# A SwiGLU kernel: splitting the first gate/up matmul by token halves, issuing the start-up loads from two queues, and changing the warm-up

## The chip, the cores and the metric

One core of one Trainium2 chip. The metric is the device time of one execution in microseconds (us), lower is better. Trace times are counted from the start of the profiled span, which is about 1.7 us shorter than the device time (123.1 us of span for a run of 124.81 us). In the trace of the kernel before, PE does the matmuls (585, with the warm-ups and its transposes), DVE copies, transposes and products (61 instructions), ACT the Silus and output copies (61, a table load among them), POOL the memsets and the identity (7), and SP only issues loads and stores; a q after a name is that engine's sequencer, on which the trace shows DMA transfers, that is, loads and stores, being issued. In the programs, PE's results are tensors declared in PSUM, and the other operands are declared in SBUF.

## The reference

```python
# x: 1 x 2048 x 512, w_gate and w_up: 512 x 1376, w_down: 1376 x 512, all bf16
def reference(x, w_gate, w_up, w_down):
    g = _silu(x @ w_gate)
    u = x @ w_up
    return (g * u) @ w_down
```

## The kernel before

The tokens are worked on in four chunks of 512. A chunk has 11 tiles of hidden columns; each tile is four gate matmuls and four up matmuls of 128x512 (four because D = 512 is contracted in steps of 128), Silu on ACT, a product on DVE, and later the down projection. The matmuls take x transposed (`xT_sb`). For chunk 0, PE transposes x itself against an identity (four token tiles of 128, called T0 to T3 here), and DVE copies each result out of PSUM. Later chunks are transposed on DVE; PE does not wait for them in the profile (its page gives 0.4 us of idle time in front of the gate matmuls, all of it for the copies of chunk 0). In front of its real work PE does *warm-ups*, and after the transposes *fillers*: matmuls on dummy data whose results nobody reads.

The parts that the change touches are all at the start:

```python
N_WARM = 26
N_FILL = 4
W_PIECES = [128, 512, 896]     # column cuts of w_gate and w_up; one DMA and one semaphore per piece
...
        @block.sync
        def _(sp):
            sp.dma_start(x_sb[:, 0, 0:2, :], x_v[:, 0, 0:2, :]).then_inc(s_xa, 16)
            sp.dma_start(x_sb[:, 0, 2:4, :], x_v[:, 0, 2:4, :]).then_inc(s_xb, 16)
            ...
            for i in range(NPC):
                ld_w(sp, "g", i)
                ld_w(sp, "u", i)
...
            pool.memset(zeros_sb[:], 0.0).then_inc(s_zero, 1)
            pool.memset(ones_sb[:], 1.0).then_inc(s_ones, 1)
...                                                     # the identity is made from ones_sb
                pe.wait_ge(s_zero, 1)
                for i in range(N_WARM):
                    pe.matmul(po[1][:, 0:P], zeros_sb[:], zeros_sb[:], start=True, stop=True)
...                                                     # T0 to T3, two PSUM buffers
                    if nT >= 2:
                        pe.wait_ge(s_xT, nT - 1)
                    for kt in range(KT):
                        ins = pe.transpose(pT[buf][:, kt * P:(kt + 1) * P], x_sb[:, 0, j, kt * P:(kt + 1) * P], ident[:])
                    ins.then_inc(s_T, 1)
                    nT += 1
                    if nT == TPC:
                        for i in range(N_FILL):
                            pe.matmul(po[1][:, 0:P], zeros_sb[:], zeros_sb[:], start=True, stop=True)
...                                                     # gate, then up, of tile ft of chunk c
                    if pi not in seen_wg:
                        pe.wait_ge(s_wg[pi], 16)
                        ...
                    if ft == 0:
                        if c == 0:
                            need = T_order.index(c * TPC + TPC - 1) + 1
                            pe.wait_ge(s_xT, need)       # all four copies
                        ...
                    for kt in range(KT):
                        ins = pe.matmul(pg[buf][0:m, :], wg_sb[:, kt, ft * P:ft * P + m],
                                        xT_sb[:, kt, c * NCH:(c + 1) * NCH], start=(kt == 0), stop=(kt == KT - 1))
```

## Time and profile before

| | before |
|---|---|
| median of 4 runs | 124.78 us (124.59 to 125.27) |
| span of the profiled run | 123.1 us |
| PE busy | 119.0 us, 97% of the span |
| first gate matmul / first up matmul | 6.45 us / 7.31 us |

The page of the kernel before: busy time per engine with its share of the span and its instructions, then shares of the chain of work that ended last.

```profile
span 123.1 us, 1467 instructions
...
PE 119.0 (97%) x585; PEld 57.7 (47%) x585; DVE 39.6 (32%) x61; ACT 36.9 (30%) x61; POOL 0.8 (1%) x7
...
PE 96%; DVE 1%; issue 0%; POOL 0%; POOLq 0%
```

PE is the bound from one end to the other in this trace: 97% busy, and 96% of the chain. From 6.45 us on, the groups of four full-size matmuls follow each other every 0.86 us. A change that leaves their number and this rate alone can only move the stretch before they run without a stop. The timeline of the kernel before shows it: start, duration, engine, line, operation, output<-inputs, count, and in brackets the idle time of the engine before it and what ended that.

```profile
0.80 0.43 SPq L153 DMA_DIRECT2D x_sb<-in_x_dram  x1
...
1.06 2.96 PE L191 MATMUL bank<-zeros_sb 128*128 128x128 bf16 x26 [1.06 <-POOL zeros_sb L178]
...
1.29 0.45 SPq L154 DMA_DIRECT2D x_sb<-in_x_dram  x1
...
3.81 1.06 PE L217 MATMUL bank<-ident,x_sb 128*128 128x128 bf16 x8
...
4.48 0.85 DVE L333 COPY xT_sb<-bank 128x512 bf16<-128x512 bf16 x2 [4.48 <-PE bank L217]
...
5.05 0.73 PE L217 MATMUL bank<-ident,x_sb 128*128 128x128 bf16 x8 [0.18 <-DVE xT_sb L333]
5.54 0.76 DVE L333 COPY xT_sb<-bank 128x512 bf16<-128x512 bf16 x2 [0.21 <-PE bank L217]
...
5.62 0.39 PE L222 MATMUL bank<-zeros_sb 128*128 128x128 bf16 x4
...
6.45 1.02 PE L241 MATMUL bank<-xT_sb,wg_sb 128*128 128x512 bf16 x4 [0.44 <-DVE xT_sb L333]
...
7.31 1.03 PE L250 MATMUL bank<-xT_sb,wu_sb 128*128 128x512 bf16 x4
...
8.17 1.03 PE L241 MATMUL bank<-xT_sb,wg_sb 128*128 128x512 bf16 x4
```

PE does 26 warm-ups, T0 and T1, waits 0.18 us for DVE to empty a PSUM buffer, does T2 and T3 and four fillers, and then waits 0.44 us for DVE's fourth copy (5.54 + 0.76 = 6.30) before the first gate matmul. From there the starts are 0.86 us apart.

### The profile page before, as it was taken

Reading aid. Unit: us, or ns where it says so; the run is one execution under the profiler, and the core shown is the slowest. Engines: PE = TensorE matmul, PEld = TensorE weight load, DVE = VectorE, ACT = ScalarE, POOL = GpSimd, SP = SyncE. Lnnn points to the kernel's source line nnn. Section 1 sums busy time; section 2 is a strip of 40 time slices with the busy share of each in tenths; the row PEclk is TensorE's granted clock in tenths of the full one; section 3 lists DMA queues with packets and bytes.
Section 4 is the critical chain, followed back from the end, with each engine's and each line's share of the span. In section 5 each row is a group of like instructions: output and inputs, shape, how many; then the busy total and the mean of one; then the engine's idle time right before and its main releaser. Section 6 shows DMA issues by size and latency. Waiting matters only on the chain.

```text
span 123.1 us, 1467 instructions
## 1 busy us (share of the span) xinstructions
PE 119.0 (97%) x585; PEld 57.7 (47%) x585; DVE 39.6 (32%) x61; ACT 36.9 (30%) x61; POOL 0.8 (1%) x7
## 2 busy tenths in 40 slices
PE   6899999999999999999999999999999999999992
PEld 6744444444444444454444444454444444454471
DVE  0423344463004443365004334438002443342001
ACT  4013332313233233311233332231125233331230
POOL 2000000000000000000000000000000000000000
PEclk9999999999999999999999999999999999999999
DMA  3999996999980000001111000000211000000121
GB/s 111 242 328 372 351 187 67 97 94 90 87 198 9 5 0 0 0 0 43 43 43 43 8 3 0 0 0 0 81 47 43 5 0 0 0 0 0 43 68 60
DMA packets 33398, 8.51 MB, mean 69 GB/s; under 512 B 26256, under 2 KB 33392, under 8 KB 33392
## 3 DMA queue, kind: packets, MB, share of 16 engines
q1 hardware_dynamic: 33248, 8.36, 30.8%
q8 instruction: 4, 0.07, 0.2%
q10 hardware_dynamic: 144, 0.07, 0.2%
q14 instruction: 2, 0.02, 0.1%
HBM read 6.32 MB, written 2.10 MB: 68 GB/s over the span
## 4 chain that ended last, share of the span: by engine, by line
PE 96%; DVE 1%; issue 0%; POOL 0%; POOLq 0%
PE bank L241 31%; PE bank L250 31%; PE bank L274 29%; PE bank L191 2%; PE bank L287 1%; PE bank L282 1%; DVE xT_sb L333 1%; PE bank L217 1%; DVE out_sb L356 0%; POOL zeros_sb L178 0%; POOLq L371 0%
## 5 line engine op out<-in xcount | busy, mean ns | idle before, releaser
L347 DVE TENSOR_TENSOR hT_sb<-bank,sg 128x512 bf16<-128x512 f32 (+1 forms) x44 | 30.4, 691 | 67.9 <-PE bank L250 67.9
L241 PE MATMUL bank<-xT_sb,wg_sb 128*128 128x512 bf16 (+1 forms) x176 | 45.2, 379 | 0.4 <-DVE xT_sb L333 0.4
L250 PE MATMUL bank<-xT_sb,wu_sb 128*128 128x512 bf16 (+1 forms) x176 | 45.2, 379 | 0.0
L305 ACT ACTIVATE sg<-bank 128x512 bf16<-128x512 f32 (+1 forms) x44 | 26.3, 597 | 51.4 <-PE bank L241 51.4
L274 PE MATMUL bank<-wd_sb,hT_sb 128*128 128x512 bf16 (+1 forms) x165 | 36.3, 379 | 0.0
L241 PEld LDWEIGHTS bank<-xT_sb,wg_sb 128*128 128x128 bf16 (+1 forms) x176 | 17.5, 100 | 20.8 <-issue 0.6
L250 PEld LDWEIGHTS bank<-xT_sb,wu_sb 128*128 128x128 bf16 (+1 forms) x176 | 17.6, 100 | 20.4
L274 PEld LDWEIGHTS bank<-wd_sb,hT_sb 128*128 128x128 bf16 (+1 forms) x165 | 16.1, 98 | 19.5
L314 ACT ACTIVATE out_sb<-bank 128x512 bf16<-128x512 f32 x15 | 9.0, 597 | 30.2 <-PE bank L274 30.2
L340 DVE STREAM_TRANSPOSE xT_sb<-xb_sb 128x512 bf16<-128x512 bf16 x12 | 7.4, 673 | 0.0
L191 PE MATMUL bank<-zeros_sb 128*128 128x128 bf16 x26 | 3.0, 313 | 1.1 <-POOL zeros_sb L178 1.1
L356 DVE CAST out_sb<-bank 128x256 bf16<-128x256 f32 x1 | 0.4, 423 | 8.9 <-PE bank L287 8.9
L191 PEld LDWEIGHTS bank<-zeros_sb 128*128 128x128 bf16 x26 | 2.7, 149 | 1.1 <-POOL zeros_sb L178 1.1
L333 DVE COPY xT_sb<-bank 128x512 bf16<-128x512 bf16 x4 | 1.6, 423 | 4.7 <-PE bank L217 4.7
L217 PE MATMUL bank<-ident,x_sb 128*128 128x128 bf16 x16 | 1.8, 275 | 0.2 <-DVE xT_sb L333 0.2
L217 PEld LDWEIGHTS bank<-ident,x_sb 128*128 128x128 bf16 x16 | 1.4, 130 | 0.5 <-issue 0.4
L294 ACT ACT_TABLE_LOAD x1 | 1.3, 1283 | 0.8 <-PEq L371 0.8
L282 PE MATMUL bank<-wd_sb,hT_sb 128*128 128x256 bf16 (+1 forms) x11 | 1.4, 272 | 0.0
L287 PE MATMUL bank<-wd_sb,hT_sb 128*128 128x256 bf16 (+1 forms) x11 | 1.4, 272 | 0.0
L282 PEld LDWEIGHTS bank<-wd_sb,hT_sb 128*128 128x128 bf16 (+1 forms) x11 | 1.1, 97 | 0.3
L287 PEld LDWEIGHTS bank<-wd_sb,hT_sb 128*128 128x128 bf16 (+1 forms) x11 | 1.1, 98 | 0.1
L316 ACT ACTIVATE out_sb<-bank 128x256 bf16<-128x256 f32 x1 | 0.4, 385 | 0.6 <-PE bank L282 0.6
(9 smaller groups left out, 1.8 us busy)
## 6 DMA issues: line engine op xcount, KB each, us to landing
out_dram<-out_sb SPq DMA_DIRECT2D x15, 128.0 KB, 1.7
xb_sb<-in_x_dram SPq DMA_DIRECT2D x12, 128.0 KB, 4.1
wd_sb<-in_w_down_dram SPq DMA_DIRECT2D x1, 1280.0 KB, 9.7
wg_sb<-in_w_gate_dram SPq DMA_DIRECT2D x2, 384.0 KB, 5.0
wu_sb<-in_w_up_dram SPq DMA_DIRECT2D x2, 384.0 KB, 5.5
x_sb<-in_x_dram SPq DMA_DIRECT2D x2, 256.0 KB, 2.7
wg_sb<-in_w_gate_dram SPq DMA_DIRECT2D x1, 480.0 KB, 6.4
wu_sb<-in_w_up_dram SPq DMA_DIRECT2D x1, 480.0 KB, 7.3
```

What stands on the lines that cost most here:

```text
L191: pe.matmul(po[1][:, 0:P], zeros_sb[:], zeros_sb[:], start=True, stop=True)
L217: ins = pe.transpose(pT[buf][:, kt * P:(kt + 1) * P], x_sb[:, 0, j, kt * P:(kt + 1) * P], ident[:])
L241: ins = pe.matmul(pg[buf][0:m, :], wg_sb[:, kt, ft * P:ft * P + m], xT_sb[:, kt, c * NCH:(c + 1) * NCH], start=(kt == 0), stop=(kt == KT - 1))
L250: ins = pe.matmul(pu[buf][0:m, :], wu_sb[:, kt, ft * P:ft * P + m], xT_sb[:, kt, c * NCH:(c + 1) * NCH], start=(kt == 0), stop=(kt == KT - 1))
L274: ins = pe.matmul(po[buf][:, :], hT_sb[0:m, ft, t * P:(t + 1) * P], wd_sb[0:m, ft, :], start=(ft == 0), stop=(ft == FT - 1))
L282: ins = pe.matmul(pTf[0][:, 0:HALF], hT_sb[0:m, ft, t * P:(t + 1) * P], wd_sb[0:m, ft, 0:HALF], start=(ft == 0), stop=(ft == FT - 1))
L287: ins = pe.matmul(pTf[1][:, HALF:D], hT_sb[0:m, ft, t * P:(t + 1) * P], wd_sb[0:m, ft, HALF:D], start=(ft == 0), stop=(ft == FT - 1))
L305: act.activation(sg_sb[nGU % NSG][0:m, :], pg[buf][0:m, :], ACT.Silu).then_inc(s_sg, 1)
L314: act.activation(out_sb[:, c, j, :], po[buf][:, :], ACT.Copy).then_inc(s_oea, 1)
L333: dve.tensor_copy(xT_sb[:, :, t * P:(t + 1) * P], src).then_inc(s_xT, 1)
L340: dve.transpose(xT_sb[:, kt, c * NCH:(c + 1) * NCH], src).then_inc(s_xTd, 1)
L347: dve.tensor_tensor(hT_sb[0:m, ft, c * NCH:(c + 1) * NCH], pu[buf][0:m, :], sg_sb[nGU % NSG][0:m, :], ALU.mult).then_inc(s_h, 1)
```

## The change

Its intent: do not wait for all of x before the first gate matmuls, and get the start-up loads going from two queues at once. The core of it (renamings, and a reshaping of views that alters nothing, are cut):

```diff
-N_WARM = 26
-N_FILL = 4
+N_WARM = 30
...
+        ones_c = nc.const_aps.tensor(1.0, [P, P], BF16)      # broadcast of a constant that the start-up code sets
...
         def _(sp):
-            sp.dma_start(x_sb[:, 0, 0:2, :], x_v[:, 0, 0:2, :]).then_inc(s_xa, 16)
-            sp.dma_start(x_sb[:, 0, 2:4, :], x_v[:, 0, 2:4, :]).then_inc(s_xb, 16)
+            sp.dma_start(x_sb[:, 0:2, :], x_v[:, 0:2, :]).then_inc(s_x0a, 16)
...
         def _(pool):
-            pool.memset(zeros_sb[:], 0.0).then_inc(s_zero, 1)
-            pool.memset(ones_sb[:], 1.0).then_inc(s_ones, 1)
-            pool.wait_ge(s_ones, 1)
...
-                pe.wait_ge(s_zero, 1)
-                for i in range(N_WARM):
-                    pe.matmul(po[1][:, 0:P], zeros_sb[:], zeros_sb[:], start=True, stop=True)
+            for i in range(N_WARM):
+                pe.matmul(po[1][:, 0:P], ones_c, ones_c, start=True, stop=True)
...
-                    if nT == TPC:
-                        for i in range(N_FILL):
-                            pe.matmul(po[1][:, 0:P], zeros_sb[:], zeros_sb[:], start=True, stop=True)
...
+                    if nGU == 0:
+                        hw_ = NCH // 2
+                        pe.wait_ge(s_wg[pi], 16)
+                        seen_wg.add(pi)
+                        for hh in range(2):
+                            pe.wait_ge(s_xTv, 2 * hh + 2)    # two copies for half 0, four for half 1
+                            for kt in range(KT):
+                                ins = pe.matmul(pg[buf][0:m, hh * hw_:(hh + 1) * hw_], wgl[:, kt],
+                                                xT_sb[:, kt, hh * hw_:(hh + 1) * hw_],
+                                                start=(kt == 0), stop=(kt == KT - 1))
+                        ins.then_inc(s_g, 1)
+                        pe.wait_ge(s_wu[pi], 16)
...                     # the same two halves for up
...
         def _(act):
+            act.dma_start(x_sb[:, 2:4, :], x_v[:, 2:4, :]).then_inc(s_x0b, 16)
             act.preload_act_table(ACT.Silu)
```

More of the change, by code (lines that the diff above doesn't have):

```diff
@@ L25, in bass_standalone__swiglu_ffn__prompt_kernel @@
     F = w_gate.shape[1]
-    assert B == 1
     P = 128
+    NCH = 512
+    assert B == 1 and S % NCH == 0 and D % P == 0 and D <= 512
     x2 = x[0]
@@ L31, in bass_standalone__swiglu_ffn__prompt_kernel @@
     KT = D // P
-    NCH = 512
     SC = S // NCH
@@ L40, in bass_standalone__swiglu_ffn__prompt_kernel @@
     HALF = D // 2
-    x_v = x2.rearrange("(c j p) d -> p c j d", p=P, j=TPC)
-    out_v = out2.rearrange("(c j p) d -> p c j d", p=P, j=TPC)
     G = NCH // 32
+    assert KT == 4 and TPC == 4
+    x_v = x2.rearrange("(t p) d -> p t d", p=P)
+    out_v = out2.rearrange("(t p) d -> p t d", p=P)
+    wg_v = w_gate.rearrange("(kt p) f -> p kt f", p=P)
+    wu_v = w_up.rearrange("(kt p) f -> p kt f", p=P)
     def piece_of(ft):
@@ L57, in sb @@
             return es.enter_context(nc.sbuf_tensor(name, shape, dt))
-        def ps(name, shape, dt):
-            return es.enter_context(nc.psum_tensor(name, shape, dt))
         def sem(name):
             return es.enter_context(nc.semaphore(name))
-        x_sb = sb("x_sb", [P, 1, TPC, D], BF16)
+        x_sb = sb("x_sb", [P, TPC, D], BF16)
         xb_sb = sb("xb_sb", [P, SC, KT, G, 32], BF16)
@@ L71, in bass_standalone__swiglu_ffn__prompt_kernel @@
         hT_sb = sb("hT_sb", [P, FT, S], BF16)
-        out_sb = sb("out_sb", [P, SC, TPC, D], BF16)
-        ones_sb = sb("ones_sb", [P, P], BF16)
+        out_sb = sb("out_sb", [P, ST, D], BF16)
         ident = sb("ident", [P, P], BF16)
-        zeros_sb = sb("zeros_sb", [P, P], BF16)
         NSG = 3
         sg_sb = [sb(f"sg{i}", [P, NCH], BF16) for i in range(NSG)]
-        banks = [ps(f"bank{i}", [P, 512], FP32) for i in range(8)]
+        ones_c = nc.const_aps.tensor(1.0, [P, P], BF16)
+        banks = [es.enter_context(nc.psum_tensor(f"bank{i}", [P, 512], FP32)) for i in range(8)]
         pg = banks[0:2]
@@ L84, in bass_standalone__swiglu_ffn__prompt_kernel @@
         pT = [b.bitcast(BF16) for b in pTf]
-        s_xa = sem("s_xa")
-        s_xb = sem("s_xb")
+        s_x0a = sem("s_x0a")
+        s_x0b = sem("s_x0b")
         s_xc = [None] + [sem(f"s_xc{c}") for c in range(1, SC)]
-        s_xTd = sem("s_xTd")
         s_wg = [sem(f"s_wg{i}") for i in range(NPC)]
@@ L93, in bass_standalone__swiglu_ffn__prompt_kernel @@
         s_ident = sem("s_ident")
-        s_ones = sem("s_ones")
-        s_zero = sem("s_zero")
         s_T = sem("s_T")
-        s_xT = sem("s_xT")
+        s_xTv = sem("s_xTv")
+        s_xTd = sem("s_xTd")
         s_g = sem("s_g")
@@ L108, in bass_standalone__swiglu_ffn__prompt_kernel @@
         block = es.enter_context(nc.Block())
-        pe_items = []
-        for t in range(TPC):
-            pe_items.append(("T", t))
+        items = [("T", j) for j in range(TPC)]
         for c in range(SC):
-            for ft in range(FT):
-                pe_items.append(("GU", c, ft))
+            items += [("GU", c, ft) for ft in range(FT)]
             for j in range(TPC):
-                pe_items.append(("D", c * TPC + j))
+                items.append(("D", c * TPC + j))
                 if c + 1 < SC:
-                    pe_items.append(("X", c + 1, j))
-        T_order = [it[1] for it in pe_items if it[0] == "T"]
-        X_order = [(it[1], it[2]) for it in pe_items if it[0] == "X"]
-        GU_order = [(it[1], it[2]) for it in pe_items if it[0] == "GU"]
-        D_order = [it[1] for it in pe_items if it[0] == "D"]
-        def x_sem(t):
-            c, j = divmod(t, TPC)
-            if c == 0:
-                return s_xa if j < 2 else s_xb
-            return s_xc[c]
-        wg_v = w_gate.rearrange("(kt p) f -> p kt f", p=P)
-        wu_v = w_up.rearrange("(kt p) f -> p kt f", p=P)
+                    items.append(("X", c + 1, j))
+        GU_list = [(it[1], it[2]) for it in items if it[0] == "GU"]
+        D_list = [it[1] for it in items if it[0] == "D"]
+        X_list = [(it[1], it[2]) for it in items if it[0] == "X"]
+        n_wd = 2 if F % P else 1
         def ld_w(eng, which, i):
@@ L140, in ld_w @@
                 eng.dma_start(wu_sb[:, :, a:b], wu_v[:, :, a:b]).then_inc(s_wu[i], 16)
-        nfull = F // P
-        n_wd = 2 if F % P else 1
-        def ld_wd(eng):
-            wd_v = w_down[0:nfull * P, :].rearrange("(ft p) d -> p ft d", p=P)
-            eng.dma_start(wd_sb[:, 0:nfull, :], wd_v).then_inc(s_wd, 16)
-            if F % P:
-                eng.dma_start(wd_sb[0:F % P, nfull, :], w_down[nfull * P:F, :]).then_inc(s_wd, 16)
         @block.sync
         def _(sp):
-            sp.dma_start(x_sb[:, 0, 0:2, :], x_v[:, 0, 0:2, :]).then_inc(s_xa, 16)
-            sp.dma_start(x_sb[:, 0, 2:4, :], x_v[:, 0, 2:4, :]).then_inc(s_xb, 16)
-            def ld_xb(c):
-                src_c = x2[c * NCH:(c + 1) * NCH, :].rearrange("(g b) (kt ii a) -> ii b kt g a", b=32, a=32, ii=4)
-                for i in range(4):
-                    sp.dma_start(xb_sb[32 * i:32 * (i + 1), c], src_c[i]).then_inc(s_xc[c], 16)
+            sp.dma_start(x_sb[:, 0:2, :], x_v[:, 0:2, :]).then_inc(s_x0a, 16)
             for i in range(NPC):
@@ L161, in _ @@
                 ld_w(sp, "u", i)
-            ld_wd(sp)
-            for c in range(1, SC):
-                ld_xb(c)
-            for i, t in enumerate(D_order):
-                c, j = divmod(t, TPC)
-                last = (i == len(D_order) - 1)
-                if last:
+            nfull = F // P
+            wd_v = w_down[0:nfull * P, :].rearrange("(ft p) d -> p ft d", p=P)
+            sp.dma_start(wd_sb[:, 0:nfull, :], wd_v).then_inc(s_wd, 16)
+            if F % P:
+                sp.dma_start(wd_sb[0:F % P, nfull, :], w_down[nfull * P:F, :]).then_inc(s_wd, 16)
+            for c in range(1, SC):
+                src_c = x2[c * NCH:(c + 1) * NCH, :].rearrange(
+                    "(g b) (kt ii a) -> ii b kt g a", b=32, a=32, ii=4)
+                for i in range(4):
+                    sp.dma_start(xb_sb[32 * i:32 * (i + 1), c], src_c[i]).then_inc(s_xc[c], 16)
+            for i, t in enumerate(D_list):
+                if i == len(D_list) - 1:
                     sp.wait_ge(s_oed, 1)
-                    sp.dma_start(out_v[:, c, j, HALF:D], out_sb[:, c, j, HALF:D]).then_inc(s_out, 16)
+                    sp.dma_start(out_v[:, t, HALF:D], out_sb[:, t, HALF:D]).then_inc(s_out, 16)
                 else:
                     sp.wait_ge(s_oea, i + 1)
-                    sp.dma_start(out_v[:, c, j, :], out_sb[:, c, j, :]).then_inc(s_out, 16)
+                    sp.dma_start(out_v[:, t, :], out_sb[:, t, :]).then_inc(s_out, 16)
             sp.wait_ge(s_out, 16 * ST)
@@ L177, in _ @@
         def _(pool):
-            pool.memset(zeros_sb[:], 0.0).then_inc(s_zero, 1)
-            pool.memset(ones_sb[:], 1.0).then_inc(s_ones, 1)
-            pool.wait_ge(s_ones, 1)
             pool.affine_select(
-                out=ident[:], in_=ones_sb[:], pattern=[[-1, P]],
+                out=ident[:], in_=ones_c, pattern=[[-1, P]],
                 compare_op=ALU.is_equal, fill=0.0, base=0, channel_multiplier=1,
@@ L187, in _ @@
         def _(pe):
-            if N_WARM:
-                pe.wait_ge(s_zero, 1)
-                for i in range(N_WARM):
-                    pe.matmul(po[1][:, 0:P], zeros_sb[:], zeros_sb[:], start=True, stop=True)
-            nT = 0
-            nGU = 0
-            nD = 0
-            h_waited = 0
-            first_T = True
-            seen_wg = set()
-            seen_wu = set()
-            seen_x = set()
-            for it in pe_items:
-                if it[0] == "X":
-                    continue
+            for i in range(N_WARM):
+                pe.matmul(po[1][:, 0:P], ones_c, ones_c, start=True, stop=True)
+            nT = nGU = nD = 0
+            h_waited = 0
+            seen_wg, seen_wu = set(), set()
+            for it in items:
                 if it[0] == "T":
-                    t = it[1]
-                    c, j = divmod(t, TPC)
-                    if first_T:
+                    j = it[1]
+                    if nT == 0:
                         pe.wait_ge(s_ident, 1)
-                        first_T = False
-                    xs = x_sem(t)
-                    if xs not in seen_x:
-                        pe.wait_ge(xs, 16)
-                        seen_x.add(xs)
-                    buf = nT % 2
+                        pe.wait_ge(s_x0a, 16)
+                    if nT == 2:
+                        pe.wait_ge(s_x0b, 16)
                     if nT >= 2:
-                        pe.wait_ge(s_xT, nT - 1)
+                        pe.wait_ge(s_xTv, nT - 1)
                     for kt in range(KT):
-                        ins = pe.transpose(pT[buf][:, kt * P:(kt + 1) * P], x_sb[:, 0, j, kt * P:(kt + 1) * P], ident[:])
+                        ins = pe.transpose(pT[nT % 2][:, kt * P:(kt + 1) * P],
+                                           x_sb[:, j, kt * P:(kt + 1) * P], ident[:])
                     ins.then_inc(s_T, 1)
                     nT += 1
-                    if nT == TPC:
-                        for i in range(N_FILL):
-                            pe.matmul(po[1][:, 0:P], zeros_sb[:], zeros_sb[:], start=True, stop=True)
                 elif it[0] == "GU":
@@ L227, in _ @@
                     pi = piece_of(ft)
+                    tok0 = c * NCH
+                    wgl = wg_sb[:, :, ft * P:ft * P + m]
+                    wul = wu_sb[:, :, ft * P:ft * P + m]
+                    if nGU == 0:
[10 more added lines that the diff above has]
+                        pe.wait_ge(s_wu[pi], 16)
+                        seen_wu.add(pi)
+                        for hh in range(2):
+                            for kt in range(KT):
+                                ins = pe.matmul(pu[buf][0:m, hh * hw_:(hh + 1) * hw_], wul[:, kt],
+                                                xT_sb[:, kt, hh * hw_:(hh + 1) * hw_],
+                                                start=(kt == 0), stop=(kt == KT - 1))
+                        ins.then_inc(s_u, 1)
+                        nGU += 1
+                        continue
+                    if c >= 1 and ft == 0:
+                        pe.wait_ge(s_xTd, X_list.index((c, KT - 1)) + 1)
                     if pi not in seen_wg:
@@ L230, in _ @@
                         seen_wg.add(pi)
-                    if ft == 0:
-                        if c == 0:
-                            need = T_order.index(c * TPC + TPC - 1) + 1
-                            pe.wait_ge(s_xT, need)
-                        else:
-                            need = X_order.index((c, KT - 1)) + 1
-                            pe.wait_ge(s_xTd, need)
                     if nGU >= 2:
@@ L240, in _ @@
                     for kt in range(KT):
-                        ins = pe.matmul(pg[buf][0:m, :], wg_sb[:, kt, ft * P:ft * P + m],
-                                        xT_sb[:, kt, c * NCH:(c + 1) * NCH], start=(kt == 0), stop=(kt == KT - 1))
+                        ins = pe.matmul(pg[buf][0:m, :], wgl[:, kt], xT_sb[:, kt, tok0:tok0 + NCH],
+                                        start=(kt == 0), stop=(kt == KT - 1))
                     ins.then_inc(s_g, 1)
@@ L249, in _ @@
                     for kt in range(KT):
-                        ins = pe.matmul(pu[buf][0:m, :], wu_sb[:, kt, ft * P:ft * P + m],
-                                        xT_sb[:, kt, c * NCH:(c + 1) * NCH], start=(kt == 0), stop=(kt == KT - 1))
+                        ins = pe.matmul(pu[buf][0:m, :], wul[:, kt], xT_sb[:, kt, tok0:tok0 + NCH],
+                                        start=(kt == 0), stop=(kt == KT - 1))
                     ins.then_inc(s_u, 1)
                     nGU += 1
-                else:
+                elif it[0] == "D":
                     t = it[1]
                     c = t // TPC
-                    buf = nD % 2
+                    last = (nD == len(D_list) - 1)
                     if nD == 0:
                         pe.wait_ge(s_wd, 16 * n_wd)
-                    last = (nD == len(D_order) - 1)
                     if nD >= 2 and not last:
@@ L265, in wait_h @@
                         nonlocal h_waited
-                        need = GU_order.index((c, ft)) + 1
+                        need = GU_list.index((c, ft)) + 1
                         if need > h_waited:
@@ L269, in wait_h @@
                             h_waited = need
-                    if not last:
+                    groups = [(po[nD % 2], 0, D)] if not last else [(pTf[0], 0, HALF), (pTf[1], HALF, D)]
+                    for (acc, c0, c1) in groups:
                         for ft in range(FT):
@@ L273, in _ @@
                             wait_h(ft)
-                            ins = pe.matmul(po[buf][:, :], hT_sb[0:m, ft, t * P:(t + 1) * P],
-                                            wd_sb[0:m, ft, :], start=(ft == 0), stop=(ft == FT - 1))
-                        ins.then_inc(s_o, 1)
-                    else:
-                        pe.wait_ge(s_xT, len(T_order))
-                        for ft in range(FT):
-                            m = fsz[ft]
-                            wait_h(ft)
-                            ins = pe.matmul(pTf[0][:, 0:HALF], hT_sb[0:m, ft, t * P:(t + 1) * P],
-                                            wd_sb[0:m, ft, 0:HALF], start=(ft == 0), stop=(ft == FT - 1))
-                        ins.then_inc(s_o, 1)
-                        for ft in range(FT):
-                            m = fsz[ft]
-                            ins = pe.matmul(pTf[1][:, HALF:D], hT_sb[0:m, ft, t * P:(t + 1) * P],
-                                            wd_sb[0:m, ft, HALF:D], start=(ft == 0), stop=(ft == FT - 1))
+                            ins = pe.matmul(acc[:, c0:c1], hT_sb[0:m, ft, t * P:(t + 1) * P],
+                                            wd_sb[0:m, ft, c0:c1], start=(ft == 0), stop=(ft == FT - 1))
                         ins.then_inc(s_o, 1)
@@ L293, in _ @@
         def _(act):
+            act.dma_start(x_sb[:, 2:4, :], x_v[:, 2:4, :]).then_inc(s_x0b, 16)
             act.preload_act_table(ACT.Silu)
-            nGU = 0
-            nD = 0
-            for it in pe_items:
+            nGU = nD = 0
+            for it in items:
                 if it[0] == "GU":
-                    c, ft = it[1], it[2]
-                    buf = nGU % 2
-                    m = fsz[ft]
+                    m = fsz[it[2]]
                     act.wait_ge(s_g, nGU + 1)
@@ L304, in _ @@
                         act.wait_ge(s_h, nGU - NSG + 1)
-                    act.activation(sg_sb[nGU % NSG][0:m, :], pg[buf][0:m, :], ACT.Silu).then_inc(s_sg, 1)
+                    act.activation(sg_sb[nGU % NSG][0:m, :], pg[nGU % 2][0:m, :], ACT.Silu).then_inc(s_sg, 1)
                     nGU += 1
@@ L308, in _ @@
                     t = it[1]
-                    c, j = divmod(t, TPC)
-                    buf = nD % 2
-                    last = (nD == len(D_order) - 1)
                     act.wait_ge(s_o, nD + 1)
-                    if not last:
-                        act.activation(out_sb[:, c, j, :], po[buf][:, :], ACT.Copy).then_inc(s_oea, 1)
+                    if nD < len(D_list) - 1:
+                        act.activation(out_sb[:, t, :], po[nD % 2][:, :], ACT.Copy).then_inc(s_oea, 1)
                     else:
-                        act.activation(out_sb[:, c, j, 0:HALF], pTf[0][:, 0:HALF], ACT.Copy).then_inc(s_oea, 1)
+                        act.activation(out_sb[:, t, 0:HALF], pTf[0][:, 0:HALF], ACT.Copy).then_inc(s_oea, 1)
                         act.wait_ge(s_oea, nD + 1)
-                        act.dma_start(out_v[:, c, j, 0:HALF], out_sb[:, c, j, 0:HALF]).then_inc(s_out2, 16)
+                        act.dma_start(out_v[:, t, 0:HALF], out_sb[:, t, 0:HALF]).then_inc(s_out2, 16)
                         act.wait_ge(s_out2, 16)
@@ L323, in _ @@
         def _(dve):
-            nT = 0
-            nGU = 0
-            nD = 0
-            for it in pe_items:
+            nT = nGU = nD = 0
+            for it in items:
                 if it[0] == "T":
-                    t = it[1]
-                    buf = nT % 2
+                    j = it[1]
                     dve.wait_ge(s_T, nT + 1)
-                    src = pT[buf][:, 0:KT * P].rearrange("p (kt s) -> p kt s", kt=KT)
-                    dve.tensor_copy(xT_sb[:, :, t * P:(t + 1) * P], src).then_inc(s_xT, 1)
+                    src = pT[nT % 2][:, 0:KT * P].rearrange("p (kt s) -> p kt s", kt=KT)
+                    dve.tensor_copy(xT_sb[:, :, j * P:(j + 1) * P], src).then_inc(s_xTv, 1)
                     nT += 1
@@ L342, in _ @@
                     c, ft = it[1], it[2]
-                    buf = nGU % 2
                     m = fsz[ft]
@@ L346, in _ @@
                     dve.wait_ge(s_sg, nGU + 1)
-                    dve.tensor_tensor(hT_sb[0:m, ft, c * NCH:(c + 1) * NCH], pu[buf][0:m, :],
+                    dve.tensor_tensor(hT_sb[0:m, ft, c * NCH:(c + 1) * NCH], pu[nGU % 2][0:m, :],
                                       sg_sb[nGU % NSG][0:m, :], ALU.mult).then_inc(s_h, 1)
@@ L350, in _ @@
                 elif it[0] == "D":
-                    t = it[1]
-                    c, j = divmod(t, TPC)
-                    last = (nD == len(D_order) - 1)
-                    if last:
+                    if nD == len(D_list) - 1:
+                        t = it[1]
                         dve.wait_ge(s_o, nD + 2)
-                        dve.tensor_copy(out_sb[:, c, j, HALF:D], pTf[1][:, HALF:D]).then_inc(s_oed, 1)
+                        dve.tensor_copy(out_sb[:, t, HALF:D], pTf[1][:, HALF:D]).then_inc(s_oed, 1)
                     nD += 1
```

## The prediction

> **What bounds the kernel now.** The page gives a span of 123.1 us, PE busy 119.0 us (97%) at full granted clock; the chain of waits is 96% PE. In the timeline, from the first gate matmul (6.45 us) on, each group of four 128x512 matmuls takes 0.86 us and nothing stalls them; after the first tile their number, shape and order do not change. So only the first 7 us can move. The chain there: zeros memset, 26 warm-up matmuls (from 1.06 us, 0.107 us start to start), transposes from 3.81 us, PSUM copies on DVE (0.42 us each; the fourth ends at 6.30), gate matmuls at 6.45, up matmuls at 7.31.
>
> **Where that start waits.** By the trace's semaphore times, the first x half landed at 3.40 us and the second at 4.08, while PE was in warm-ups until 3.81. The first weight pieces landed at 5.4 (gate) and 6.15 us (up). So loads were not last; the warm-up count and then the transpose/copy ping-pong were. Loading earlier has almost no direct value.
>
> **What the change does.**
> 1. Split first tile: gate on tokens 0-255 needs only copies 1 and 2 (done 5.33 us). It can run while copies 3 and 4 finish, where before PE ran four fillers and waited 0.44 us. Eight 256-wide matmuls cost about 0.11 us each (the last output's: 11 in 1.21 us), so both halves cost the same 0.86 us. Four of them, 0.43 us, move into the hole. Gain about 0.4 us.
> 2. Warm-ups: 30 for 26, on the constant, so no memset in front: start near 0.82 instead of 1.06 us, 4 x 0.107 = 0.43 us more work. Transposes start near 4.02 instead of 3.81. Loss about 0.2 us. The fillers (0.2 us) were inside a wait: no gain.
> 3. The second half of x goes out on the ACT queue at 0.8 instead of 1.29 us; weights are issued 0.5 us earlier. [...] DMA share is about 1.0 from 2.5 to 3.5 us. The first half now shares bandwidth and may land as late as 4.0 us, near the new end of the warm-ups: 0 to 0.1 us of loss. Weights arrive 0.2 to 0.4 us sooner, off the chain.
> 4. The table load on ACT moves back 0.5 us; it is needed only at 7.5 us. Free.
>
> Net: up matmuls start near 7.1 instead of 7.31 us; 0.2 us off, from a kernel whose runs spread over 0.7 us.
>
> **Prediction:** 124.5 us, range 123.9 to 125.1. Faster by over 2%: 0.01; within 2%: 0.98; slower by over 2%: 0.01.
>
> **What would show it.** Right: first-half gate matmuls near 5.8 us, PE idle of at most 0.4 us before the second half, up matmuls near 7.1, steady 0.86 us groups afterwards, PE busy almost unchanged. Wrong: transposes waiting long for x (step 3), warm-ups spaced more than 0.107 us (step 2), or the second gate tile waiting for weights.
>
> **What would make it wrong.** The broadcast constant may load as weights more slowly than a full tile: 30 warm-ups at 0.15 us would cost over 1 us. The PE clock: matmul spacing falls from 0.107 to 0.056 us near 5.3 us. [...] An earlier or later release shifts the start by some tenths of a us.

Two passages that no trace or run of this case supports are cut from it and marked. No term of the forecast's sum is among them: it came to about 0.4 us of gain less about 0.2 us of loss, that is, 0.2 us off. In its last paragraph, the 0.15 us per warm-up was a supposition (e2 measured 0.107 us), and the shift by some tenths of a us an estimate of mine (in the trace of e1 a later rise of the matmul rate cost about 0.3 us).

## The result, and the profile after

| | before | after |
|---|---|---|
| median | 125.02 us (16 runs, 124.59 to 125.27) | 124.64 us (11 runs, 124.32 to 124.91) |
| ratio, 95% interval | | 0.9978 (0.9966 to 0.9991) |
| span of the profiled run | 123.1 us | 122.8 us |
| first gate / first up matmul | 6.45 / 7.31 us | 5.80 / 7.02 us |

Ratios here and below are the mean time of one kernel's runs over that of the other's in the same rounds, so they are not quite the ratio of the medians quoted. Executions over 1.5% slower than the fastest of the same kernel are left out of the means. The change is a small gain, clear of the noise, within 2%.

The page of the changed kernel, the same lines:

```profile
span 122.8 us, 1481 instructions
...
PE 119.2 (97%) x593; PEld 58.6 (48%) x593; DVE 39.6 (32%) x61; ACT 36.9 (30%) x61; POOL 0.5 (0%) x5
...
PE 96%; DVE 1%; issue 0%
```

The timeline of the changed kernel:

```profile
0.80 0.43 SPq L127 DMA_DIRECT2D x_sb<-in_x_dram  x1
...
0.81 0.49 ACTq L256 DMA_DIRECT2D x_sb<-in_x_dram  x1
0.84 3.36 PE L160 MATMUL bank<-const-bfloat16-1.0 128*128 128x128 bf16 x30 [0.84 <-PEq L322]
...
4.04 1.01 PE L175 MATMUL bank<-ident,x_sb 128*128 128x128 bf16 x8
...
4.66 0.85 DVE L287 COPY xT_sb<-bank 128x512 bf16<-128x512 bf16 x2 [4.66 <-PE bank L175]
...
5.23 0.74 PE L175 MATMUL bank<-ident,x_sb 128*128 128x128 bf16 x8 [0.18 <-DVE xT_sb L287]
...
5.76 0.76 DVE L287 COPY xT_sb<-bank 128x512 bf16<-128x512 bf16 x2 [0.25 <-PE bank L175]
5.80 0.60 PE L194 MATMUL bank<-xT_sb,wg_sb 128*128 128x256 bf16 x4
...
6.57 0.61 PE L194 MATMUL bank<-xT_sb,wg_sb 128*128 128x256 bf16 x4 [0.17 <-DVE xT_sb L287]
...
7.02 1.04 PE L202 MATMUL bank<-xT_sb,wu_sb 128*128 128x256 bf16 x8
...
7.89 1.03 PE L216 MATMUL bank<-xT_sb,wg_sb 128*128 128x512 bf16 x4
```

The transposes start 0.23 us later (4.04 for 3.81), and the copies are late by about as much (the fourth ends at 6.52 for 6.30). The first gate half then runs at 5.80 us where the fillers were, and only the second half waits for the fourth copy. The up matmuls start 0.50 us after the end of the fourth copy, where before they started 1.01 us after it: less the 0.22 us of delay, that makes the 0.29 us by which they are earlier (7.02 for 7.31). So is the second tile (7.89 for 8.17). The spans differ by the same 0.3 us (123.1 and 122.8). So in these two traces the whole difference lies before the second tile.

What the page does not show is when each load landed, which the trace's semaphore events give, here the last of the 16 increments of each in us. The runs named e1 to e12 are the experiments of the next section.

```
load                    before  after |  e1    e2    e4   (x on SP only) |  e3    e5   e8   e12 (x on SP and ACT)
x, first half            3.40   3.90  | 3.48  3.57  3.49                 | 4.00  3.92  4.02  3.92
x, second half           4.08   4.38  | 4.52  4.26  4.17                 | 4.38  4.37  4.39  4.36
gate weights, piece 0    5.40   4.87  | 5.91  5.29  5.79                 | 4.86  4.86  4.89  4.83
up weights, piece 0      6.14   6.32  | 6.40  6.57  6.32                 | 5.40  5.33  5.84  5.89
gate weights, piece 1    7.28   7.38  | 7.47  7.95  7.39                 | 7.00  6.96  7.31  7.29
up weights, piece 1      8.51   8.47  | 8.55  9.10  8.53                 | 8.46  8.24  8.54  8.85
```

In these traces, issuing x from two queues made the first half land later (3.90 to 4.02 us for 3.40 to 3.57) and the first gate weights 0.4 to 1.1 us earlier. The second half landed at 4.36 to 4.39 us, later than in three of the four traces with x on SP alone.

### The profile page after: what moved, and what is told of

Its sections match the earlier page's. It is cut to its first block, busy times and chain, and to the rows that moved or that the text cites. A ratio compares the mean times of both kernels' runs of the same rounds, so it can differ in the third digit from the quotient of the medians.

```text
span 122.8 us, 1481 instructions
## 1 busy us (share of the span) xinstructions
PE 119.2 (97%) x593; PEld 58.6 (48%) x593; DVE 39.6 (32%) x61; ACT 36.9 (30%) x61; POOL 0.5 (0%) x5
## 3 DMA queue, kind: packets, MB, share of 16 engines
HBM read 6.32 MB, written 2.10 MB: 69 GB/s over the span
## 4 chain that ended last, share of the span: by engine, by line
PE 96%; DVE 1%; issue 0%
PE bank L249 31%; PE bank L216 30%; PE bank L225 30%; PE bank L160 3%; DVE xT_sb L287 1%; PE bank L175 1%; PE bank L202 1%; PE bank L194 0%; DVE out_sb L307 0%
## 5 line engine op out<-in xcount | busy, mean ns | idle before, releaser
L216 PE MATMUL bank<-xT_sb,wg_sb 128*128 128x512 bf16 (+1 forms) x172 | 44.1, 379 | 0.0
L225 PE MATMUL bank<-xT_sb,wu_sb 128*128 128x512 bf16 (+1 forms) x172 | 44.1, 379 | 0.0
L249 PE MATMUL bank<-wd_sb,hT_sb 128*128 128x512 bf16 (+3 forms) x187 | 38.7, 366 | 0.0
L160 PE MATMUL bank<-const-bfloat16-1.0 128*128 128x128 bf16 x30 | 3.4, 309 | 0.8 <-PEq L322 0.8
L160 PEld LDWEIGHTS bank<-const-bfloat16-1.0 128*128 128x128 bf16 x30 | 3.1, 144 | 0.8 <-issue 0.8
L194 PE MATMUL bank<-xT_sb,wg_sb 128*128 128x256 bf16 x8 | 1.2, 274 | 0.2 <-DVE xT_sb L287 0.2
L202 PE MATMUL bank<-xT_sb,wu_sb 128*128 128x256 bf16 x8 | 1.0, 272 | 0.0
L194 PEld LDWEIGHTS bank<-xT_sb,wg_sb 128*128 128x128 bf16 x8 | 0.7, 98 | 0.5 <-DVE xT_sb L287 0.4
L202 PEld LDWEIGHTS bank<-xT_sb,wu_sb 128*128 128x128 bf16 x8 | 0.8, 98 | 0.1
```

Source lines behind the costliest of these rows:

```text
L160: pe.matmul(po[1][:, 0:P], ones_c, ones_c, start=True, stop=True)
L194: ins = pe.matmul(pg[buf][0:m, hh * hw_:(hh + 1) * hw_], wgl[:, kt], xT_sb[:, kt, hh * hw_:(hh + 1) * hw_], start=(kt == 0), stop=(kt == K ...
L202: ins = pe.matmul(pu[buf][0:m, hh * hw_:(hh + 1) * hw_], wul[:, kt], xT_sb[:, kt, hh * hw_:(hh + 1) * hw_], start=(kt == 0), stop=(kt == K ...
L216: ins = pe.matmul(pg[buf][0:m, :], wgl[:, kt], xT_sb[:, kt, tok0:tok0 + NCH], start=(kt == 0), stop=(kt == KT - 1))
L225: ins = pe.matmul(pu[buf][0:m, :], wul[:, kt], xT_sb[:, kt, tok0:tok0 + NCH], start=(kt == 0), stop=(kt == KT - 1))
L249: ins = pe.matmul(acc[:, c0:c1], hT_sb[0:m, ft, t * P:(t + 1) * P], wd_sb[0:m, ft, c0:c1], start=(ft == 0), stop=(ft == FT - 1))
```

## The experiments

The theory at the start: the split earns about 0.43 us by filling the wait for the last copies, and half of it is given back because the transposes start later. The rivals: the gain is from the parallel loads; or from the earlier warm-up. All kernels gave correct results. Each was timed in five rounds, six runs with the profiled one, beside 11 runs of the kernel before on the same chip.

| run | what it is | ratio to before (95%) | range, us |
|---|---|---|---|
| e1 | before + split alone | 1.0001 (0.9983 to 1.0018) | 124.58 to 125.33 |
| e2 | before + new warm-up alone | 1.0017 (1.0005 to 1.0030) | 124.93 to 125.23 |
| e3 | before + x on two queues alone | 1.0013 (0.9997 to 1.0029) | 124.85 to 127.00 |
| e4 | after, x on SP only | 0.9997 (0.9976 to 1.0017) | 124.34 to 125.35 |
| e5 | before + split + x on two queues | 0.9977 (0.9959 to 0.9995) | 124.46 to 124.95 |
| e6 | after, larger first weight pieces | 0.9986 (0.9966 to 1.0007) | 124.47 to 125.33 |
| e7 | after, no warm-up | 1.0043 (1.0020 to 1.0066) | 125.06 to 125.94 |
| e8 | after, 24 warm-ups | 0.9983 (0.9944 to 1.0022) | 124.31 to 126.24 |
| e9 | after, x in quarters, 26 warm-ups | 1.0019 (0.9988 to 1.0049) | 124.41 to 126.86 |
| e10 | e9 + smaller second weight piece | 0.9995 (0.9975 to 1.0015) | 124.49 to 125.21 |
| e11 | after, 26 warm-ups, smaller second piece | 0.9975 (0.9960 to 0.9990) | 124.41 to 126.57 |
| e12 | after, again | 0.9979 (0.9963 to 0.9994) | 124.36 to 124.85 |

### e1, the split alone

```diff
-N_FILL = 4
+N_FILL = 0
...
+                    if nGU == 0:      # the two-half branch of the change, everything else as before
```

> The kernel before with the split of the first tile alone (no fillers, 26 zero warm-ups, both x halves on SP). My theory: the split earns 0.43 us and the longer warm-up gives half of it back. Then the first gate half starts near 5.62 us, the up matmuls near 6.85 instead of 7.31, and the time is 0.45 us less than before: ratio about 0.9964. The second up tile is then needed near 8.6 us, when its weights have just landed (8.51 before), so some of it may be lost to that. Rival: the gain of the change comes from the parallel loads, and the split is worth nothing: ratio 1.000, up matmuls at 7.3 us.

Measured: ratio 1.0001, a miss for my theory in the time. The timeline of e1 shows why its profiled run gained little:

```profile
3.81 1.06 PE L217 MATMUL bank<-ident,x_sb 128*128 128x128 bf16 x8
...
5.05 1.01 PE L217 MATMUL bank<-ident,x_sb 128*128 128x128 bf16 x8 [0.18 <-DVE xT_sb L354]
5.67 0.85 DVE L354 COPY xT_sb<-bank 128x512 bf16<-128x512 bf16 x2 [0.34 <-PE bank L217]
...
5.95 1.16 PEld L235 LDWEIGHTS bank<-xT_sb,wg_sb 128*128 128x128 bf16 x8 [0.16 <-DMA wg_sb<-in_w_gate_dram]
5.96 1.44 PE L235 MATMUL bank<-xT_sb,wg_sb 128*128 128x256 bf16 x8
...
7.23 1.04 PE L243 MATMUL bank<-xT_sb,wu_sb 128*128 128x256 bf16 x8
```

The gate half started at 5.96 us instead of 5.62, just after its weights landed (5.91), and eight gate matmuls took 1.44 us against 1.04 us for eight up matmuls of the same size. In the instruction times, the matmuls were 0.213 us apart until 6.8 us and 0.109 after: this run still had the slow matmul rate, which in the trace of before had ended near 5.2 us. Two things met here, late weights and a late rise of the rate, and the second was the larger. The last transpose began at 5.75 us and took 0.107 us, so that the weights held PE up by at most 0.10 us (5.96 for 5.86); the rest of the 0.38 us by which the up matmuls missed the forecast (7.23 for 6.85) is the slow rate. The other five runs have no trace.

### e2, the new warm-up alone

```diff
-N_WARM = 26
+N_WARM = 30
...
-                pe.wait_ge(s_zero, 1)
...
-                    pe.matmul(po[1][:, 0:P], zeros_sb[:], zeros_sb[:], start=True, stop=True)
+                    pe.matmul(po[1][:, 0:P], ones_c, ones_c, start=True, stop=True)   # no memsets; fillers likewise
```

> The kernel before with the warm-ups of the change alone: 30 matmuls on the broadcast constant, no memsets, fillers and everything else as before. My theory: warm-ups start near 0.84 us, still 0.107 us apart, transposes start near 4.03 instead of 3.81, up matmuls near 7.53 instead of 7.31, time 0.2 us more: ratio 1.0018. Rival: the earlier start of the warm-ups is itself a gain [...]: ratio under 1.000.

Measured: 1.0017, transposes from 3.99 us, spacing 0.107 us. As expected: by itself this part costs 0.2 us. In this trace the broadcast constant was no slower as weights than the full tile of zeros in the trace of before (0.107 us in both).

### e3, x on two queues alone

```diff
-            sp.dma_start(x_sb[:, 0, 2:4, :], x_v[:, 0, 2:4, :]).then_inc(s_xb, 16)     # in the SP program
...
+            act.dma_start(x_sb[:, 0, 2:4, :], x_v[:, 0, 2:4, :]).then_inc(s_xb, 16)    # ahead of the table load
```

> The kernel before with the second half of x issued on the ACT queue, nothing else. My theory: loading in parallel is no gain, because the first half shares the DMA engines with the second: it lands at 3.9 instead of 3.40 us, so the transposes start near 3.95 to 4.0 instead of 3.81 and the time is 0 to 0.2 us more, ratio 1.000 to 1.0016. Rival (the intent of the change): parallel loads bring the start forward by some tenths of a us, ratio 0.998 or less.

Its first transposes:

```profile
4.14 1.01 PE L216 MATMUL bank<-ident,x_sb 128*128 128x128 bf16 x8
```

Measured: 1.0013; the first half landed at 4.00 us and the transposes started at 4.14 us. The sign is that of my theory, but the interval (0.9997 to 1.0029) also holds no change; of the rival's gain there is nothing. One of the six runs took 127.00 us; see e8.

### e4, the changed kernel with x on SP alone

```diff
+            sp.dma_start(x_sb[:, 2:4, :], x_v[:, 2:4, :]).then_inc(s_x0b, 16)     # behind the first half
...
-            act.dma_start(x_sb[:, 2:4, :], x_v[:, 2:4, :]).then_inc(s_x0b, 16)
```

> The changed kernel with both x halves back on the SP queue, one after the other. My theory: same time as the changed kernel (ratio to before about 0.9978), since its transposes wait for the 30 warm-ups until 4.03 us, and x has landed either way; first half near 3.40 us, second near 4.1 us. Rival: the parallel load is a needed part, and the time goes back towards the kernel before, ratio near 1.000.

Measured: 0.9997, with an interval that holds both expectations. Its timeline, of a run that happened to be its fastest (124.34 us), is the useful part:

```profile
3.87 0.61 PE L176 MATMUL bank<-ident,x_sb 128*128 128x128 bf16 x8
...
5.84 1.05 PE L195 MATMUL bank<-xT_sb,wg_sb 128*128 128x256 bf16 x8 [0.34 <-DMA wg_sb<-in_w_gate_dram]
...
7.60 1.03 PE L217 MATMUL bank<-xT_sb,wg_sb 128*128 128x512 bf16 x4
...
8.58 1.04 PE L226 MATMUL bank<-xT_sb,wu_sb 128*128 128x512 bf16 x4
```

Here the fast rate came at 3.7 us, the transposes took 0.61 instead of 1.01 us, and PE then waited for the *gate weights*, and once more for the second up piece (landed 8.53, matmul at 8.58, where 8.46 would have followed without a wait). So in this trace, where the front of the chain was quicker, PE waited for the weights. What that cost is an estimate of mine from these times: the fourth copy ended at 6.04 us, so that without the wait the up matmuls could have begun near 6.54 instead of 6.73 (0.50 us after that copy, as in the trace of after), and with the second wait some 0.3 us in all.

### e5, the split with the two-queue load, but the old warm-up

> The kernel before with the split and with the second x half on ACT, but with its own 26 zero warm-ups behind the memset. The split alone measured 1.0001 and the ACT load alone 1.0013. Theory A (the two need each other): issuing x from two queues lets the first gate weights land at 4.9 instead of 5.3 to 5.9 us, so the first gate half no longer waits for them, and together they give 0.997 to 0.9985, at least the whole gain of the change. Theory B (the effects add, warm-ups on the constant are the missing part): ratio about 1.0014.

The edit is that of e1 and e3 together. Measured: 0.9977, theory A. The additive expectation 1.0014 lies outside the interval (it is itself a sum of two measurements; the difference of 0.0037 is a little larger than the uncertainty of all three together, about 0.003). What theory A says of the time is borne out; that the weights are the reason is not shown by it. Its timeline is that of the changed kernel to within 0.1 us:

```profile
4.06 0.92 PE L216 MATMUL bank<-ident,x_sb 128*128 128x128 bf16 x8
...
5.74 0.60 PE L234 MATMUL bank<-xT_sb,wg_sb 128*128 128x256 bf16 x4
6.49 0.61 PE L234 MATMUL bank<-xT_sb,wg_sb 128*128 128x256 bf16 x4 [0.15 <-DVE xT_sb L354]
6.94 1.04 PE L242 MATMUL bank<-xT_sb,wu_sb 128*128 128x256 bf16 x8
```

With 26 warm-ups the transposes still start at 4.06 us, because x landed at 3.92. So in the changed kernel the longer warm-up costs nothing beyond what the x load costs: both end near 3.9 us, and the later of the two counts, not their sum.

### e6, larger first weight pieces

```diff
-W_PIECES = [128, 512, 896]
+W_PIECES = [256, 640, 1024]
```

> The changed kernel with weight pieces cut at 256, 640, 1024 columns instead of 128, 512, 896. If the 256-byte rows of the first pieces are what keeps the loads slow near 4 to 5 us, the first gate piece, twice as large, lands no later than 5.5 us, and the second tile has no weights to wait for any more; the kernel is as fast as the changed one or up to 0.2 us faster: ratio to before 0.996 to 0.998. If the loads are bound by bytes, the first gate piece lands near 5.6 us and the up piece near 6.8 us, and the ratio is 0.998 to 1.000.

(The slow loads near 4 to 5 us, in the trace of before: 129 GB/s from 4.0 to 4.5 us and 141 from 4.5 to 5.0, against 334 and 328 in the two half microseconds from 2.5 us.)

Its first up matmuls:

```profile
7.19 1.05 PE L202 MATMUL bank<-xT_sb,wu_sb 128*128 128x256 bf16 x8
```

Measured: 0.9986. The first gate piece, twice the bytes in 512-byte rows instead of 256, landed at 5.05 us against 4.87, early as the first theory said. But the first up piece, also twice the bytes, landed at 7.14 us, later even than the second theory said, and the up matmuls, which could have followed at 6.91, started at 7.19. The interval holds both theories; a gain over the changed kernel is not seen.

### e7 and e8, fewer warm-ups

```diff
-N_WARM = 30
+N_WARM = 0        # e7
+N_WARM = 24       # e8
```

> The changed kernel without any warm-up matmul. The traces so far show the matmul spacing fall from 107 to 56 ns between 3.7 and 6.9 us, at a different time in each, after 2.9 to 5.8 us of matmuls. If the release needs that much matmul activity, without warm-ups PE starts near 3.95 us with the transposes and stays slow until between 7 and 10.5 us: 1 to 2.5 us more than the changed kernel, ratio to before 1.006 to 1.018. If the warm-ups only delayed the transposes, the time is the same or less, ratio 0.996 to 0.998.

> The changed kernel with 24 warm-ups instead of 30. My theory in the prediction was that 30 warm-ups delay the transposes by 0.2 us. But the first x half landed at 3.9 us in the changed kernel, so with 24 warm-ups (ending near 3.4 us) the transposes start no earlier than about 4.0 us: same time as the changed kernel, ratio to before 0.997 to 0.9985. Rival: the warm-ups are what delays it, ratio 0.995 or less.

e7 measured 1.0043. Its matmuls stayed at the slow rate until about 9.0 us, in the predicted stretch; the loss was smaller than I had expected (1.006 to 1.018), some 0.8 us against the changed kernel (125.48 against 124.64 us).

e8 measured 0.9983, and as expected its transposes waited for x, not for the warm-ups. But its runs fall in two groups: 124.31, 124.43, 124.51, 124.63, and 125.97, 126.24. The profiled one is the 125.97:

```profile
4.16 1.01 PE L175 MATMUL bank<-ident,x_sb 128*128 128x128 bf16 x8 [0.60 <-DMA x_sb<-in_x_dram]
...
6.16 1.91 PE L194 MATMUL bank<-xT_sb,wg_sb 128*128 128x256 bf16 x8
7.87 1.60 PE L202 MATMUL bank<-xT_sb,wu_sb 128*128 128x256 bf16 x8
9.30 1.03 PE L216 MATMUL bank<-xT_sb,wg_sb 128*128 128x512 bf16 x4
```

Against the changed kernel the second tile starts 1.4 us later (9.30 for 7.89), nearly all of it because of the slow rate, which lasted until 9.0 us, some 3.5 us longer than in the trace of the changed kernel. The 24 warm-ups ended with a hole in front of the transposes (0.91 us from the last warm-up's start to the first transpose's, with 0.60 us of PE idle). The 126.24 us run has no trace.

### e9 to e11, looking for a better version, and e12

```diff
# e9: tiles 0 and 2 of x on SP, tiles 1 and 3 on ACT, with the first gate weights behind them on ACT; N_WARM = 26
-            sp.dma_start(x_sb[:, 0:2, :], x_v[:, 0:2, :]).then_inc(s_x0a, 16)
+            sp.dma_start(x_sb[:, 0:1, :], x_v[:, 0:1, :]).then_inc(s_x0a, 16)
+            sp.dma_start(x_sb[:, 2:3, :], x_v[:, 2:3, :]).then_inc(s_x0b, 16)
-            act.dma_start(x_sb[:, 2:4, :], x_v[:, 2:4, :]).then_inc(s_x0b, 16)
+            act.dma_start(x_sb[:, 1:2, :], x_v[:, 1:2, :]).then_inc(s_x0a, 16)
+            act.dma_start(x_sb[:, 3:4, :], x_v[:, 3:4, :]).then_inc(s_x0b, 16)
+            ld_w(act, "g", 0)
# e10: e9 with W_PIECES = [128, 384, 896]
# e11: the changed kernel with N_WARM = 26 and W_PIECES = [128, 384, 896]
# e12: the changed kernel
```

> A version that should beat both: the changed kernel with x loaded in four quarters, tiles 0 and 2 on SP, tiles 1 and 3 on ACT, the first gate weights behind them on ACT, and 26 warm-ups on the constant (ending near 3.62 us). If the first two quarters (the bytes of one half) land near 3.5 us, the transposes start near 3.65 instead of 4.03 us and the up matmuls near 6.65 instead of 7.02; the second up tile then waits for its weights (landing near 8.4 us, wanted near 8.4). Ratio to before 0.9955 to 0.997. Rival: sharing the DMA engines between queues delays the first two quarters as it delayed the half, to 3.9 us: ratio 0.997 to 0.999.

> The same with weight pieces cut at 128, 384, 896, so that the second pieces are 256 columns and land before the second tile wants them. If the weights are what stops the quarters version, this is 0.1 to 0.3 us faster than it (ratio to before 0.994 to 0.996); if the clock release or x is, the two are alike.

> The changed kernel with 26 warm-ups (ending near 3.62 us) and pieces cut at 128, 384, 896. The first x half still lands near 3.9 us, so the transposes start near 4.0 us and the time is that of the changed kernel, ratio 0.997 to 0.9985. The hole of 0.4 us in front of the transposes is about half of that with 24 warm-ups, where two runs of six were 1.5 us slower; if the hole is what makes the clock release late, such runs are rarer here.

> The changed kernel unchanged, a second sample beside the others on this chip. Ratio to before 0.9966 to 0.9991 as recorded; PE has no hole in front of the transposes beyond 0.15 us and no run over 125.4 us.

e9 failed (1.0019, and two of six runs near 126.8 us; its profiled run is one of those, so that its trace is not that of a usual run). e10 failed too (0.9995). The quarters did what was hoped for x: in e10 the first two landed at 3.53 us and the transposes began at 3.67. But the timeline of e10 shows the price:

```profile
3.67 1.01 PE L177 MATMUL bank<-ident,x_sb 128*128 128x128 bf16 x8
...
6.52 1.05 PE L196 MATMUL bank<-xT_sb,wg_sb 128*128 128x256 bf16 x8 [0.77 <-DMA wg_sb<-in_w_gate_dram]
```

With gate weights on ACT and up weights on SP at the same time, both landed late and close together (6.47 and 6.19 us); the gate weights, needed first, had been at 4.87 us. Part of that may be the later issue, at 1.73 us behind two quarters of x instead of 1.29. It looks like what was measured for x, where of two loads side by side the one needed first came late too (3.90 for 3.40 us). This was not varied alone.

That e10 is faster than e9, as the first half of its expectation has it, is not clear of the noise: the intervals overlap. e11 measured 0.9975 with one run of 126.57 us (the hole was 0.57 us between starts), e12 0.9979, the result once more, with no run over 124.85 us; its spacing in front of the transposes was 0.18 us, a little over the 0.15 expected. In its trace the second up piece landed late (8.85 us) and was waited for. e11 is not told apart from the changed kernel. No version that I ran beats the changed kernel.

## Why the prediction was right, and where its steps were not

The forecast was 124.5 us and a gain of 0.2%; measured were 124.64 us and 0.22%. The stated range (123.9 to 125.1) also holds the time of the kernel before, 125.02 us, so the hit in time says little by itself; the forecast start times say more. The mechanism of the split held in the trace. That the sum came out so close is in part luck, as the third and fourth point show. Point by point:

- **Where the time can come from.** Right: PE at 97%, and the whole difference before the second tile.
- **The split (gain 0.4 us).** Right in the trace: the first gate half started at 5.80 us (5.8 forecast) and the up matmuls at 7.02 (7.1 forecast). Not right as a step by itself: alone it gave 1.0001 (e1); with the two-queue load 0.9977 (e5).
- **The warm-up (loss 0.2 us).** Right alone (e2: 1.0017, transposes at 3.99 us), and the transposes started at 4.04 us as forecast (4.02). But in the changed kernel this is luck: x landed at 3.90 us, and with 26 warm-ups beside the same x load the transposes start at 4.06 (e5) and 4.03 (e11), as with 30 (4.04, and 4.06 in e12). Two delays of the same size lay on top of each other, so the longer warm-up cost nothing there, and I had named too small a share for x (0 to 0.1 us; alone it measured 0.13%, about 0.16 us, with an interval that holds no change).
- **"Loading earlier has almost no direct value."** The runs speak against this step. In the trace of before it holds, for the chain there ended at the fourth copy at 6.30 us. The split moves the first need for gate weights forward by 0.65 us, into the stretch where they land. With x on SP alone they landed between 5.29 and 5.91 us in four traces, and in the trace of e4 PE waited for them; with two queues at 4.77 to 5.00 us in the seven traces with this order of loads and this first piece (after, e3, e5, e7, e8, e11, e12). The three parts alone give 1.0001, 1.0017 and 1.0013, all no gain, and multiplied 1.0031; together they measured 0.9978, further away than the noise of about 0.003. So the effects did not add here. That the early weights are the reason is argued from these times; how far it carries is said under what stays open.
- **"Weights arrive 0.2 to 0.4 us sooner."** Only the first gate piece did (4.87 for 5.40). The first up piece and the second gate piece landed later than before in that trace (6.32 for 6.14, 7.38 for 7.28); in e3, e5, e8 and e12 the first up piece came 0.25 to 0.8 us earlier.
- **Which load shares.** Right in these traces: in that of the changed kernel, the packet records have the SP half of x moving from 1.89 to 3.45 us and the ACT half from 2.51 to 3.88 us, with a DMA share of 1.05 and 1.07 in the two half microseconds from 2.5 us, and the first x half landed 0.5 us later (3.90 for 3.40).
- **The clock as what could make it wrong.** The matmul rate is the largest source of spread that the traces show: spacing of 0.107 us at first, 0.056 us later, at a time that differs from run to run. The faster spacing came 2.9 us (e4: 0.84 to 3.7) to 5.7 us (e1: 1.06 to 6.8) after the first matmul in the traces of the table with no hole in front of the transposes, and 8.2 and 9.3 us after it in e8 and e9, where PE had stood idle in between.

| trace | spacing, last warm-up to first transpose | fast rate from about | this run |
|---|---|---|---|
| e4 | none to speak of | 3.7 us | 124.34 us |
| before | 0.11 us | 5.2 us | 124.81 us |
| after | 0.15 us | 5.5 us | 124.53 us |
| e2 | 0.11 us | 6.3 us | 125.19 us |
| e1 | 0.11 us | 6.8 us | 124.77 us |
| e8 | 0.91 us | 9.0 us | 125.97 us |
| e9 | 0.38 us | 10.2 us | 126.82 us |

The page's own row of granted clock, from which the prediction took "full granted clock", does not show this: on the page of before it is 9 (90% or more) in all 40 slices, the first ones too, where the matmuls are 0.107 us apart (the trace's clock record begins at 5.23 us). What sets the time of the rise is not shown by these runs. It was not the split that made it late in e1: the timelines of e1 and of before have the same starts up to the second pair of transposes (3.81 and 5.05 us), and the edit first acts behind those, when the rate had risen in before (5.2 us) and had not in e1. In e8 the late rise comes with a hole of 0.91 us between starts; in e9 with one of 0.38 us and a wait of 0.70 us for gate weights.

What stays open: the interval of e1 just overlaps that of e5, and e4 is not told apart from the changed kernel in time (0.9997 against 0.9979, overlapping). Each of the two pairs favours the two-queue load, by 0.0024 and by 0.0019, with an uncertainty of about 0.0025. Why the split alone gained nothing is not settled. Late weights cost at most 0.10 us in the trace of e1 and some 0.3 us in that of e4, and in the trace of after weights at 5.91 us would have cost nothing, since the second half waited for the fourth copy until 6.57 us; a late rise of the rate accounts for e1's profiled run but not for its five others, which have no trace. Also open is whether the hole is the cause of the runs that were 1.7 to 2.5 us slower than the fastest of their kernel. All runs above 125.9 us, save one without any warm-up, came from kernels whose trace shows a spacing of 0.36 us or more in front of the transposes (e3, e8, e9, e11; e5 had none in six runs), and none from the kernel before or the changed one; e8 and e9 show the late rise of the rate in the trace (9.0 and 10.2 us). In e9 the wait for gate weights may be the cause as well as the hole; I did not vary the hole alone. If it is so, then the four additional warm-ups of the change, which I counted as a loss, are what covers the later landing of x.

## What to carry to other kernels

When PE is busy from end to end, work the start-up as a chain of arrivals: list for each step when its data landed, its slack, and what would be next if it came earlier; a step with 0.5 us of slack becomes the one to wait for as soon as the need for it moves forward by that much. Parts of such a change should be tried together as well as alone, for each may measure nothing without the other. Look at what a second queue does to the load that is needed first: here the first half of x landed 0.5 us later for it. And where a warm-up precedes a load, compare its end with the landing of the load before shortening it, and look at every timed run, not only the median.
